# Fused attention and two-stage MLP: decode operations spread over a pair's period, phi one step later, an interleaved drain, and an earlier start for the last weight decodes

## The chip, the core and the metric

The kernel runs on one core of a Trainium2 chip. Five engines work side by side: TensorE (PE, with its weight loads listed as PEld), VectorE (DVE), ScalarE (ACT), GpSimd (POOL) and SyncE (SP), whose queue here issues nearly all transfers. The metric is device time in microseconds of one execution, lower is better.

## The reference, cut to what matters

```python
# q, k, v: (4, 8, 576, 64) f32; M_prev: (4, 8, 64, 64); z_prev: (4, 8, 64)
scores = causal(scale * q @ k.T)
a = exp(scores - scores.max(-1)); a /= a.sum(-1) + 1e-9
local = a @ v
q_p = phi(q)                      # phi(x) = where(x > 0, x, exp(x) - 1) + 1
mem_out = (q_p @ M_prev) / (q_p . z_prev + 1e-6)
x = g * mem_out + (1 - g) * local # g = sigmoid(beta), then x: (2304, 512)

h = x @ w_in                      # 512 -> 2048, float64 weights
x = (h * tanh(softplus(h))) @ w_out

a = x @ w1; b = x @ w2            # 512 -> 1024, float64 weights
out = (a * b @ w3) @ w_out2       # 1024 -> 1024 -> 512
```

The weights arrive in float64. The kernel turns each of their 128x512 tiles into float32 on the chip: this is what "decode" means below.

## The kernel before, in words

**Attention.** 32 heads are taken as 16 pairs. The loop over `p` (L514) has 17 turns: in turn `p` the scores and the softmax of pair `p` are made, and the probabilities of pair `p - 1` are transposed and multiplied by v (`pt_g`, `pv`). Scores come in blocks of rows: `s_blocks` for block 3, block 2, blocks 0 and 1, and `s_last` for the last 64 rows of both heads. For each block PE writes scores to a PSUM tile `psA`, DVE takes the masked maximum (`maxed`, L373), and ACT the exponential with its row sum (`expd`, L378). `normed` (L363 to L368) scales the rows, some on DVE and some on POOL (`ON_POOL`). `pt_g` transposes on PE into `psF`, and ACT copies the result out (L430). `pv` collects the pair's output in one `psX` and one `psF` bank; ACT copies the high part out and DVE subtracts for the low part (`sub`, L79).

**phi.** `prep_phi(p)` makes phi(q) of a pair, divided by its norm and times the gate: an exponential on ACT (L330), a GpSimd add (L331), a DVE combine (L332), a GpSimd product with z (L334), a DVE sum (L338), small steps (L339 to L341), and a GpSimd scale (L344). `trans_phi(p)` transposes the result on PE into two `psX` banks and copies it out on ACT (L351). Both were called for pair `p + 1` at the end of turn `p`, after `pv`.

**Decode.** `decode` fetches a raw tile ("draw", 512 KB, on SP's queue), runs six DVE operations on it (L113, L115, L117, L120, L124, L126) and one GpSimd addition (L131). Its user then splits the result into a rounded part (L76) and a rest (L79 or L160), both on GpSimd. `lq0` lists the eight tiles of the first quarter of `w_in` and `w_out`. `run(lq0, 1)` stood in turns 3, 6, 9 and 12, with one raw buffer; the other four tiles were decoded in turn 16, with a decoder of their own.

**First MLP.** It runs by quarters `g` of the hidden width and by chunks `n` of 384 tokens: 24 units. `emit_h` makes h in two `psA` tiles, applies tanh, arctan and sin on ACT (L477 to L485) and multiplies by h on DVE (L487). `emit_x2` multiplies by `w_out` and adds to `x2`. The first two units, (0, 0) and (0, 1), stand in turn 16 beside the last pair's work. Decodes of the next quarter run beside the units.

**Last quarter and second MLP.** Beside the units of the last quarter `fold` decodes `w3` tile by tile and multiplies it with the decoded `w_out2`, 17 steps in all. The second halves of `w2` and `w1` (eight tiles, two to a step, `rest`) are written to the place of the second half of x (`w_slot(1)`), one step in the last `emit_x2` and three beside the first blocks of the second MLP (`k < 3`). At `k == 4` the decoder's memory is given back, and the second set of x tiles (`x2s`, filled by L731 and L732) takes it.

**Order.** The framework's planner puts every engine's instructions in one fixed order when the kernel is built; emission order is its priority, and an instruction that has all it needs may be taken ahead of earlier-emitted ones. `issue_after(i)` only forbids instructions of `i`'s engine from going ahead of `i`. `in_turn` uses it to keep PE's work in emission order for turns 1 to 15.

Of the kernel before, what the change touches and what calls it, by code (L numbers as in the profile page):

```python
# [21 lines left out]
def fused_kernel(ctx: ExitStack, tc, q, k, v, M_prev, z_prev, beta, w_in, w_out, w1, w2, w3, w_out2, out):  # L22
    nc = tc.nc
# [78 lines left out]

    def decode(srcs):

        V = nc.vector
        ts = []
        for src in srcs:
            r = dec["pool"].tile([128, dec["w"], 2], I32, tag="draw", name="draw", bufs=dec["raw"])
            dm(out=r.rearrange("p n t -> p (n t)"), in_=src)
            a = dec_tile("da")  # L110
            ts.append((r[:, :, 0], r[:, :, 1], a, a.bitcast(I32), r.rearrange("p n t -> p (n t)").bitcast(F32)))
        for lw, hw, a, ai, _ in ts:
            V.tensor_scalar(out=ai, in0=hw, scalar1=0x7FFFFFFF, scalar2=None, op0=ALU.bitwise_and)  # L113
        for lw, hw, a, ai, _ in ts:
            V.tensor_scalar(out=a, in0=a, scalar1=2.0 ** -15, scalar2=122879.9921875, op0=ALU.max, op1=ALU.min)  # L115
        for lw, hw, a, ai, _ in ts:
            V.tensor_scalar(out=ai, in0=ai, scalar1=3, scalar2=0x3FFFFFF8,  # L117
                            op0=ALU.logical_shift_left, op1=ALU.bitwise_and)
        for lw, hw, a, ai, _ in ts:
            V.scalar_tensor_tensor(  # L120
                out=ai, in0=hw, scalar=-0x40000000, in1=ai, op0=ALU.bitwise_and, op1=ALU.bitwise_or
            )
        for lw, hw, a, ai, _ in ts:
            V.tensor_scalar(out=hw, in0=ai, scalar1=-0x800000, scalar2=None, op0=ALU.bitwise_and)  # L124
        for lw, hw, a, ai, _ in ts:
            V.scalar_tensor_tensor(  # L126
                out=lw.bitcast(F32), in0=lw.bitcast(U32), scalar=2.0 ** -52, in1=hw.bitcast(F32),
                op0=ALU.mult, op1=ALU.mult,
            )
        for lw, hw, a, ai, _ in ts:  # L130
            nc.gpsimd.tensor_tensor(out=a, in0=a, in1=lw.bitcast(F32), op=ALU.add)  # L131
            yield a, _
# [81 lines left out]
    decoder(at, 1, 1)  # L214
# [107 lines left out]
    def prep_phi(p):  # L322
# [15 lines left out]
        nc.vector.tensor_reduce(out=dn, in_=qz, axis=mybir.AxisListType.X, op=ALU.add)  # L338
# [10 lines left out]
    def trans_phi(p):  # L349
        t = ap_.tile([128, S], F32, tag="phi", name="phi", bufs=2)  # L350
        trans(st[p]["e"], lambda cs, o: nc.scalar.copy(out=t[:, cs], in_=o))  # L351
# [19 lines left out]

    def maxed(s, o, m, init, a):
        nc.vector.tensor_tensor_reduce(  # L373
            out=s, in0=o, in1=m, op0=ALU.add, op1=ALU.min, scale=-scale, scalar=init, accum_out=a,
        )
# [45 lines left out]
    def pt_g(p, gi):  # L421
# [8 lines left out]
        nc.scalar.copy(out=t[:, 0:n], in_=o[:, 0:n])  # L430

    def pv(p):
# [16 lines left out]
        for o, q0, q1 in ((pm, 0, 512), (pl, 512, S)):  # L449
            x = xl[b // 2][:, :, c, S * (b % 2) + q0:S * (b % 2) + q1]  # L450
            nc.scalar.copy(out=x[:, 0], in_=o[:, 0:q1 - q0])
            sub(x[:, 1], o[:, 0:q1 - q0], x[:, 0])
# [3 lines left out]
    def emit_h(u, beside=iter(())):  # L456
# [7 lines left out]
        for m in range(KQ):  # L464
# [9 lines left out]
            if m == 1:  # L474
                steps(beside, 1)
# [4 lines left out]
        first = nc.scalar.activation(out=d, in_=y[1][:, 1, 0:1], func=AF.Sin, scale=0.0)  # L480
# [3 lines left out]
        for i in range(2):  # L484
            nc.scalar.activation(out=y[i], in_=y[i], func=AF.Sin, scale=-2.0, bias=halfpi)  # L485
            for j in range(2):
                nc.vector.tensor_tensor(out=y[i][:, j], in0=y[i][:, j], in1=hp[2 * i + j], op=ALU.mult)  # L487
        return y
# [23 lines left out]
    lq0 = load_quarter(0)  # L512
    pre = predecode()
    for p in range(NPAIR + 1):  # L514

        now, old, new = p < NPAIR, p > 0, p + 1 < NPAIR
        ordered[0] = 1 <= p < NPAIR
        if old:
            ensure_x((p - 1) // (2 * NP))
        if not now:  # L520
            ek.close()
            wps[0] = wk.enter_context(tc.tile_pool(name="wp", bufs=1, side="right"))
            lk = ExitStack()
            decoder(lk, 2, 2, side="right")
        if p + 2 < NPAIR:
            load_pair(p + 2)
            load_v(p + 2)
        if now:
# [294 lines left out]
```

## Time and profile before

| what | value |
|---|---|
| median of 3 runs | 1025.31 us (1024.01 to 1026.53) |
| the profiled execution | 1024.95 us |
| its span | 1023.2 us |
| PE busy | 977.8 us, 96% |
| DVE, ACT, POOL busy | 60%, 49%, 33% |

The span goes from the first to the last instruction of the program. A busy PE is not a PE at its peak, since matmuls are pipelined; idle time on an engine costs something only where the chain of work that ends last goes through it. Times in views of the trace are counted from the start of the span.

### The profile page before, as it was taken

The page shows a single profiled execution, that of the slowest core. Times are in us where ns is not written, and L with a number is a line of the kernel's source. Part 1 is how long each engine was busy: PE and PEld are TensorE (multiplying, and loading weights), DVE is VectorE, ACT ScalarE, POOL GpSimd, SP SyncE. Part 2 cuts the span into 40 slices and gives each one's busy share as a digit, 9 for nine tenths or more (in the row PEclk, how much of TensorE's full clock was granted, in tenths as well). Part 3 has the DMA queues.
Part 4 walks back from the last instruction along what each step waited for, and adds up shares of the span by engine and source line. Part 5 has one row for each costly group of instructions (what it writes and reads, how often), then busy time and mean ns, then how long its engine had stood idle before and what let it go on. Part 6 is the DMA issues. An engine that isn't in the chain of part 4 may idle for free.

```text
span 1023.2 us, 15086 instructions
## 1 busy us (share of the span) xinstructions
PE 977.8 (96%) x5584; PEld 829.1 (81%) x5584; DVE 612.0 (60%) x1364; ACT 500.7 (49%) x1016; POOL 339.0 (33%) x345
## 2 busy tenths in 40 slices
PE   5888999999899999999999999999979999999998
PEld 2555555566799999999999999988758888888897
DVE  4887667667685759885987567667973121121111
ACT  5577888885655555556565544442313221221212
POOL 6675555433555254544454112112540000000000
PEclk9899999999999999999999999999999999999999
DMA  7343333311232124223331662222410000100101
GB/s 157 96 110 71 71 87 74 77 27 42 103 124 80 65 83 145 98 89 106 121 103 63 247 232 80 75 78 101 156 41 1 21 21 1 42 1 1 42 1 62
DMA packets 93626, 81.73 MB, mean 80 GB/s; under 512 B 68720, under 2 KB 72816, under 8 KB 93552
## 3 DMA queue, kind: packets, MB, share of 16 engines
q1 hardware_dynamic: 92224, 80.44, 25.3%
q8 instruction: 44, 0.72, 0.3%
q10 hardware_dynamic: 1328, 0.33, 0.2%
q14 instruction: 30, 0.25, 0.1%
HBM read 65.54 MB, written 15.20 MB: 79 GB/s over the span
## 4 chain that ended last, share of the span: by engine, by line
PE 71%; DVE 12%; ACT 11%; DMA 2%; POOL 2%; issue 2%; SPq 0%; POOLq 0%; ACTq 0%; DVEq 0%
PE psA L63 37%; PE psX L63 16%; PE psF L63 14%; ACT s L378 5%; ACT pt L430 3%; DVE s L368 2%; PE psF L66 2%; DMA draw<-in_moe_w_dram 1%; DVE da L120 1%; PE psX L66 1%; DVE xt L79 1%; POOL da L131 1%; DVE draw L126 1%; DVE da L117 1%; DVE s L373 1%
## 5 line engine op out<-in xcount | busy, mean ns | idle before, releaser
L63 PE MATMUL psA<-xt,wqt 128*128 128x384 f32 x1152 | 207.5, 335 | 0.2
L131 POOL TENSOR_TENSOR da<-da,draw 128x512 f32<-128x512 f32 x72 | 102.2, 1426 | 312.8 <-DVE draw L126 261.9
L63 PEld LDWEIGHTS psA<-xt,wqt 128*128 128x128 f32 x1152 | 200.0, 188 | 2.4 <-DVE y L487 0.8
L63 PE MATMUL psX<-gh,wqt 128*128 128x384 f32 x480 | 122.4, 335 | 1.1 <-DVE x L604 1.1
L749 DVE TENSOR_TENSOR bs<-bs,psA 128x512 f32<-128x512 f32 (+1 forms) x40 | 25.3, 633 | 160.0 <-ACT bs L748 160.0
L63 PE MATMUL psA<-x2h,w12t 128*128 128x512 f32 (+1 forms) x384 | 107.1, 356 | 6.9 <-DVE bs L749 4.6
L748 ACT COPY bs<-psA 128x512 f32<-128x512 f32 (+1 forms) x40 | 21.8, 545 | 162.1 <-PE psA L63 152.2
L378 ACT ACTIVATE s<-s,acc 128x512 f32<-128x512 f32 (+2 forms) x144 | 85.5, 603 | 12.8 <-DVE acc L373 12.7
L63 PE MATMUL psA<-x2s,w12t 128*128 128x512 f32 x384 | 89.6, 389 | 0.0
L63 PEld LDWEIGHTS psX<-gh,wqt 128*128 128x128 f32 x480 | 86.9, 188 | 2.3 <-DVE x L604 1.4
L477 ACT ACTIVATE y<-psA 128x384 f32<-128x384 f32 x96 | 42.0, 490 | 91.1 <-PE psA L63 91.0
L63 PEld LDWEIGHTS psA<-x2h,w12t 128*128 128x128 f32 x384 | 68.3, 189 | 20.7 <-DVE bs L749 5.0
L63 PEld LDWEIGHTS psA<-x2s,w12t 128*128 128x128 f32 x384 | 72.1, 188 | 14.9
L373 DVE CUSTOM_DVE_ANT_0 s<-psA,mask 128x512 f32<-128x512 f32 (+2 forms) x144 | 63.4, 483 | 34.4 <-PE psA L63 34.3
L63 PE MATMUL psX<-gl,wqt 128*128 128x384 f32 x240 | 80.3, 335 | 0.0
L66 PEld LDWEIGHTS psF<-ident,s 128*128 128x128 f32 x400 | 46.3, 147 | 40.8 <-ACT pt L430 24.8
L63 PE MATMUL psF<-gh,wqt 128*128 128x384 f32 x288 | 73.1, 334 | 0.0
L66 PE MATMUL psF<-ident,s 128*128 128x128 f32 x400 | 63.2, 292 | 9.9 <-ACT pt L430 7.5
L487 DVE TENSOR_TENSOR y<-y,psA 128x384 f32<-128x384 f32 x96 | 48.7, 549 | 34.9 <-ACT y L485 34.9
L63 PE MATMUL psA<-room,w12t 128*128 128x512 f32 (+1 forms) x192 | 68.0, 354 | 0.0
L368 POOL TENSOR_SCALAR s<-s,sum,ogp 128x128 f32<-128x128 f32 (+1 forms) x64 | 53.1, 840 | 37.2 <-DVE sum L364 37.2
L430 ACT COPY pt<-psF 128x512 f32<-128x512 f32 (+1 forms) x112 | 56.8, 546 | 16.0 <-PE psF L66 16.0
(114 smaller groups left out, 1878.3 us busy)
## 6 DMA issues: line engine op xcount, KB each, us to landing
draw<-in_moe_w_dram SPq DMA_DIRECT2D x32, 512.0 KB, 3.8
draw<-in_moe_w_out_dram SPq DMA_DIRECT2D x24, 512.0 KB, 3.5
draw<-in_moe_w_in_dram SPq DMA_DIRECT2D x16, 512.0 KB, 4.0
out_dram<-ob SPq DMA_DIRECT2D x18, 256.0 KB, 2.0
raw<-in_q_dram SPq DMA_DIRECT2D x32, 128.0 KB, 2.8
raw<-in_v_dram SPq DMA_DIRECT2D x32, 128.0 KB, 2.6
o_dram<-draw SPq DMA_DIRECT2D x8, 512.0 KB, 2.8
w_dram<-draw SPq DMA_DIRECT2D x8, 512.0 KB, 2.8
```

The lines of the kernel that those rows point to most:

```text
L63: tail[0] = nc.tensor.matmul(o, lhsT=l, rhs=r, start=start, stop=stop).ins
L66: tail[0] = nc.tensor.transpose(o, src, ident).ins
L79: return (eng or nc.vector).tensor_tensor(out=dst, in0=src, in1=f(hi), op=ALU.subtract)
L131: nc.gpsimd.tensor_tensor(out=a, in0=a, in1=lw.bitcast(F32), op=ALU.add)
L368: (nc.gpsimd if x in ON_POOL else nc.vector).tensor_scalar(out=s, in0=s, scalar1=d["sum"][:, x:x + 1], scalar2=og[:, x:x + 1], op0=ALU.mul ...
L373: nc.vector.tensor_tensor_reduce(out=s, in0=o, in1=m, op0=ALU.add, op1=ALU.min, scale=-scale, scalar=init, accum_out=a,)
L378: nc.scalar.activation(out=s, in_=s, func=AF.Exp, scale=-1.0, bias=a, accum_out=r)
L430: nc.scalar.copy(out=t[:, 0:n], in_=o[:, 0:n])
L477: nc.scalar.activation(out=y[m // 2][:, m % 2], in_=hp[m], func=AF.Tanh, scale=0.5)
L487: nc.vector.tensor_tensor(out=y[i][:, j], in0=y[i][:, j], in1=hp[2 * i + j], op=ALU.mult)
L748: nc.scalar.copy(out=bs, in_=pb)
L749: nc.vector.tensor_tensor(out=bs, in0=bs, in1=pa, op=ALU.mult)
```

## The change

- Decodes in attention: one tile of `lq0` in each of turns 4 to 11, fetched one turn ahead, with two raw buffers. Its six DVE operations are issued by `drip`: one after each of the four calls that make scores, the rest at the turn's end, each behind the last masked maximum emitted so far (`taken[0]`). The four decodes of turn 16 are gone.
- phi: `prep_phi(p + 1)` stays at the end of turn `p`, but its DVE operations stand behind the turn's last masked maximum, and its sum (L338) behind `pv`'s low part (`split_x[0]`). `trans_phi` is called a turn later, and its second half goes to `psF` instead of `psX`. phi of pair 0 is made at the end of turn 0 and transposed in turn 1. The last `normed` of a turn stands behind `split_x[0]` too.
- Drain (turn 16): PE's work follows emission order here as well. `emit_h` becomes a generator, and the four column blocks of unit (0, 0) are interleaved with the seven transposition groups of the last pair; the table load for sin stands behind the last copy of `pt_g`.
- Last quarter: `rest` begins in unit (3, 5), in `emit_x2` of (3, 4), alternating with `fold` (`both`): one step there, two in the last `emit_x2`, one beside the second MLP.

```diff
-    def decode(srcs):
+    def decode_ops(r):
...
+        ops = [ ... six DVE operations, one GpSimd addition, unchanged ... ]
+        return ops, a, flat
+
+    def fetch(src):
+        r = dec["pool"].tile([128, dec["w"], 2], I32, tag="draw", name="draw", bufs=dec["raw"])
+        dm(out=r.rearrange("p n t -> p (n t)"), in_=src)
+        return r
...
-    decoder(at, 1, 1)
+    decoder(at, 2, 1)
...
-    def trans(src, evac):
-        for c0, c1 in ((0, 256), (256, S)):
-            pt = psX()
+    def trans(src, evac, tags="XX"):
+        for tag, (c0, c1) in zip(tags, ((0, 256), (256, S))):
+            pt = bank(tag)
...
-        nc.vector.tensor_reduce(out=dn, in_=qz, axis=mybir.AxisListType.X, op=ALU.add)
+        with ExitStack() as k_:
+            if split_x[0] is not None:
+                k_.enter_context(tc.issue_after(split_x[0]))
+            nc.vector.tensor_reduce(out=dn, in_=qz, axis=mybir.AxisListType.X, op=ALU.add)
...
+    def drip(n):
+        if not parts and ahead:
+            r, done = ahead.pop(0)
+            ops, a, flat = decode_ops(r)
+            def last():
+                ops[6]()
+                done(a, flat)
+            parts.extend(ops[0:6] + [last])
+        with tc.issue_after(taken[0]):
+            for op in parts[:n]:
+                op()
+        del parts[:n]
...
-        ordered[0] = 1 <= p < NPAIR
+        ordered[0] = 1 <= p
...
-            lk = ExitStack()
-            decoder(lk, 2, 2, side="right")
+            h0 = h_steps((0, 0))
...
+        decodes = 4 <= p < 12
+        if 3 <= p < 11:
+            fetch_next()
         if now:
             in_turn(s_blocks, p, (3,))
+            if decodes:
+                drip(1)
         else:
-            split = split_y((0, 0), emit_h((0, 0)))
+            in_turn(next, h0)
...
-        if not now:
-            run(lq0, 2)
-            run(lq0, 2)
+            if not now:
+                in_turn(next, h0)
...
-        if p in (3, 6, 9, 12):
-            run(lq0, 1)
...
+        if now:
+            with ExitStack() as k_:
+                if old:
+                    k_.enter_context(tc.issue_after(split_x[0]))
+                normed(p, [(4, None)])
+            if decodes:
+                drip(7)
         if new:
-            prep_phi(p + 1)
-            in_turn(trans_phi, p + 1)
-        if now:
-            normed(p, [(4, None)])
+            with tc.issue_after(taken[0]):
+                prep_phi(p + 1)
+        if now and p > 0:
+            in_turn(trans_phi, p)
...
+        if last and n == NCH - 1:
+            rest = by_two(second_half(w_slot(1)))
+            beside = both(folding, rest)
...
-    rest = by_two(second_half(w_slot(1)))
-    emit_x2(prev, islice(rest, 1))
+    emit_x2(prev, rest)
```

## Rows read from the trace of the kernel before

**Rows 1.** Page, part 1: busy time and share of each engine.

```profile
PE 977.8 (96%) x5584; PEld 829.1 (81%) x5584; DVE 612.0 (60%) x1364; ACT 500.7 (49%) x1016; POOL 339.0 (33%) x345
```

**Rows 2.** Windows of attention, cut where a pair's first masked maximum starts.

```profile
core 0: us, PE busy (x) PEld busy (x) DVE busy (x) ACT busy (x) POOL busy (x), PEclk, DMA share, GB/s
12.70:26.20 13.50, 7.20 (x30) 3.86 (x31) 9.96 (x38) 9.00 (x27) 10.24 (x12) 0.83 0.73 166
26.20:97.30 71.10, 60.07 (x416) 38.29 (x416) 58.54 (x169) 47.84 (x137) 47.53 (x53) 0.89 0.37 93
82.00:97.30 15.30, 12.94 (x93) 8.51 (x90) 9.71 (x37) 11.07 (x33) 10.19 (x12) 0.89 0.31 72
97.30:208.80 111.50, 105.86 (x818) 65.96 (x816) 77.42 (x281) 93.67 (x273) 60.08 (x72) 1.00 0.34 77
208.80:221.90 13.10, 12.40 (x97) 7.46 (x96) 8.95 (x35) 10.92 (x33) 6.81 (x8) 1.00 0.10 23
221.90:236.30 14.40, 13.60 (x104) 8.43 (x105) 7.93 (x32) 11.08 (x33) 3.81 (x5) 1.00 0.03 7
```

**Rows 3.** Source line L113, first decode operation: durations min/median/max, first and last start.

```profile
L113 DVE TENSOR_SCALAR da<-draw x4: 422/426/434, 30.1 to 76.6; 128x512 int32<-128x512 int32 x4
```

**Rows 4.** Timeline of one steady pair: start, duration, operation, idle before and releaser.

```profile
119.78 0.17 DVE L363 TENSOR_SCALAR sum<-sum 128x8 f32<-128x8 f32 x1 [0.61 <-ACT s L378]
...
122.68 0.55 PE L66 MATMUL psX<-ident,phie 128*128 128x128 f32 x3 [0.35 <-DVE xt L79]
...
124.22 1.09 PE L66 MATMUL psF<-ident,s 128*128 128x128 f32 x8
124.41 0.83 DVE L332 SCALAR_TENSOR_TENSOR phie<-phie,phit 128x640 f32<-128x640 f32 x1 [1.17 <-ACT phie L330]
...
125.16 0.68 DVE L373 CUSTOM_DVE_ANT_0 s<-psA,mask 128x512 f32<-128x512 f32 x1
```

**Rows 5.** Timeline of the start: first scores, pair 0's phi, first masked maximum.

```profile
8.57 3.17 PE L63 MATMUL psA<-kt,qt 64*128 64x512 f32 x8
...
12.01 0.82 DVE L338 TENSOR_REDUCE dn<-qz 128x10 f32<-128x640 f32 x1 [3.12 <-POOL qz L334]
...
12.74 0.68 DVE L373 CUSTOM_DVE_ANT_0 s<-psA,mask 128x512 f32<-128x512 f32 x1
```

**Rows 6.** Groups by line, 0 to 420 us: decode's operations, count, busy, mean ns.

```profile
L131 POOL TENSOR_TENSOR da<-da,draw 128x512 f32<-128x512 f32 x27 | 38.8, 1445 | 90.7 <-DVE draw L126 73.6 <-issue 11.8 <-PE psA L63 5.3
...
L79 POOL TENSOR_TENSOR wqt<-da,wqt 128x512 fp32r<-128x512 f32 x20 | 25.8, 1301 | 0.5
...
L120 DVE SCALAR_TENSOR_TENSOR da<-draw,da 128x512 int32<-128x512 int32 x28 | 21.8, 799 | 0.2
...
L76 POOL TENSOR_SCALAR wqt<-da 128x512 fp32r<-128x512 f32 x20 | 12.9, 653 | 0.5
...
L113 DVE TENSOR_SCALAR da<-draw 128x512 int32<-128x512 int32 x28 | 12.7, 471 | 13.3 <-DMA draw<-in_moe_w_out_dram 5.1 <-POOL wqt L79 4.8 <-POOL s L368 1.8
```

**Rows 7.** Timeline in pair 1, GpSimd and VectorE at the same time.

```profile
31.45 1.65 POOL L334 TENSOR_TENSOR qz<-phie,zr 128x640 f32<-128x640 f32 x1 [1.71 <-DVE phie L332]
31.61 1.51 DVE L341 TENSOR_TENSOR dn<-dn,gates 128x10 f32<-128x10 f32 x1
```

**Rows 8.** Windows of the drain and of the passage to the second MLP.

```profile
677.00:717.00 40.00, 38.94 (x202) 34.74 (x202) 28.30 (x54) 11.99 (x22) 8.42 (x7) 1.00 0.25 86
717.00:768.00 51.00, 43.79 (x182) 32.91 (x182) 44.13 (x61) 13.40 (x25) 25.73 (x21) 1.00 0.29 98
248.90:277.50 28.60, 26.01 (x159) 21.69 (x160) 19.38 (x35) 14.33 (x25) 14.25 (x12) 0.94 0.22 75
```

**Rows 9.** Timeline of the drain: copies of transposed probabilities, then h's multiply.

```profile
257.67 1.08 ACT L430 COPY pt<-psF 128x512 f32<-128x512 f32 x2
...
264.69 0.55 DVE L487 TENSOR_TENSOR y<-y,psA 128x384 f32<-128x384 f32 x1
```

**Rows 10.** Chain that ended last, in order of time: start, duration, work.

```profile
243.28 4.22 PE psX L63 x20
...
285.85 8.32 PE psA L63 x48
```

**Rows 11.** Waits: engine and line, waited for, total, times, longest.

```profile
ACT x2s L731 <- POOL w12t L79: 16.9, 1, 16.9
```

More of the change, by code (lines that the diff above doesn't have):

```diff
@@ L134, in run, with decode @@
+    def decode(srcs):
+        ts = [decode_ops(fetch(src)) for src in srcs]
+        for i in range(6):
+            for ops, _, _ in ts:
+                ops[i]()
+        for ops, a, flat in ts:
+            ops[6]()
+            yield a, flat
     def run(jobs, n):
@@ L487, in emit_h @@
                 nc.vector.tensor_tensor(out=y[i][:, j], in0=y[i][:, j], in1=hp[2 * i + j], op=ALU.mult)
+        yield y
+    def emit_h(u, beside=iter(())):
+        for m, y in enumerate(h_steps(u)):
+            if m == 1:
+                steps(beside, 1)
         return y
@@ L512, in fused_kernel, with fetch_next @@
     lq0 = load_quarter(0)
+    ahead = []
+    parts = []
+    def fetch_next():
+        for src, done in islice(lq0, 1):
+            ahead.append((fetch(src), done))
+    def drip(n):
[3 more added lines that the diff above has]
+            def last():
+                ops[6]()
+                done(a, flat)
[4 more added lines that the diff above has]
+        del parts[:n]
     pre = predecode()
@@ L545, in fused_kernel @@
             in_turn(pt_g, p - 1, 2)
+            if not now:
+                in_turn(next, h0)
         if new:
@@ L551, in fused_kernel @@
             in_turn(s_blocks, p, (0, 1))
+            if decodes:
+                drip(1)
         if new:
@@ L556, in fused_kernel @@
             in_turn(pt_g, p - 1, 6)
+            if not now:
+                in_turn(next, h0)
+        if p == 1:
+            in_turn(trans_phi, 0)
         if now:
             in_turn(s_last, p)
+            if decodes:
+                drip(1)
             normed(p, [(i, e) for e in range(2) for i in range(4)])
         if p == 0:
-            in_turn(trans_phi, 0)
-        if p in (3, 6, 9, 12):
-            run(lq0, 1)
+            with tc.issue_after(taken[0]):
+                prep_phi(0)
         if old:
@@ L566, in fused_kernel @@
         if not now:
+            split = split_y((0, 0), next(h0))
             early = {(0, 1): emit_h((0, 1))}
-        if new:
-            prep_phi(p + 1)
-            in_turn(trans_phi, p + 1)
-        if now:
-            normed(p, [(4, None)])
-    lk.close()
+        if now:
+            with ExitStack() as k_:
+                if old:
+                    k_.enter_context(tc.issue_after(split_x[0]))
+                normed(p, [(4, None)])
+            if decodes:
+                drip(7)
+        if new:
+            with tc.issue_after(taken[0]):
+                prep_phi(p + 1)
+        if now and p > 0:
+            in_turn(trans_phi, p)
     at.close()
@@ L665, in w_slot, with both @@
         return t
+    def both(a, b):
+        while True:
+            next(a, None)
+            yield
+            next(b, None)
+            next(a, None)
+            yield
     folding = fold()
@@ L681, in fused_kernel @@
             w_slot(0)
+        if last and n == NCH - 1:
+            rest = by_two(second_half(w_slot(1)))
+            beside = both(folding, rest)
         if prev is not None:
-            with tc.issue_after(emit_x2(prev, folding if last and n > 0 else pre0)):
+            with tc.issue_after(emit_x2(prev, beside if last and n > 0 else pre0)):
                 split = split_y(u, y)
```

67 lines of the change are left out of this document (33 added, 34 removed).

## Prediction, made before the changed kernel was run

> **What bounds the kernel now.** I read the page's engine shares first, then the chain of work that ended last, then windows by stage, and the timeline only where the windows show loss. PE is busy nearly all of the span [rows 1], and from the drain to the end the chain is matmul after matmul; there only PE's gaps can be won. Attention is different. With no decode in it, a pair takes 111.5 / 8 = 13.94 us, and ACT, DVE and POOL are busy 11.7, 9.7 and 7.5 us of that [rows 2]: no engine is full, the chain hops from ACT to DVE to PE and back. The four pairs between 26.2 and 97.3 us took 71.1, so 17.8 each, 15.3 us more than four steady ones. All four decodes that attention holds started there, from 30.1 to 76.6 us [rows 3], though they were emitted in turns 3 to 12: the planner took them as early as their data allowed. DVE is busy 58.54 us in these four pairs against 38.7 in four steady ones, and the granted clock is 0.89 instead of 1.00 [rows 2]. So this stretch is where an order for the decodes can matter.
>
> Two smaller losses stand elsewhere. The drain, 28.6 us, holds two units' h of 8.32 us each [rows 8, 10] plus the last pair's transposes and products. The passage to the second MLP leaves PE idle 51.0 - 43.8 = 7.2 us, with DVE busy 44.1 of 51 [rows 8].
>
> **The start.** PE's first scores begin at 8.57; eight matmuls take 3.17 us, so the first block, half of them, ends near 10.2. Yet the first maximum starts at 12.74, behind pair 0's phi sum, which waited for GpSimd [rows 5]. That sum is now emitted behind the maxima. I put the first maximum at 10.5: -2.2 us. Turn 0 also loses phi's DVE work for two pairs, but has half a pair's work on other engines anyway: 13.5 becomes 12.5 (estimate), -1.0.
>
> **Pairs 1 to 3, now without decodes.** They took 82.0 - 26.2 = 55.8 us. Two at 13.75 (below) and one at 15.5: the start still leaves PE mostly idle (7.2 of 13.5 us [rows 2]), so a stretch at the lower clock level remains likely. The price of 1.5 is from the pair at 82.0, which had no more DVE work than a steady one, a clock of 0.89, and 1.35 us more time [rows 2]. Sum 43.0, so -12.8.
>
> **phi a turn later.** Two things go from a steady pair's path. PE stood 0.35 us before the second phi transposition, because its bank was the one that DVE was still reading; `psF` is free by then. And phi's combine, 0.83 us, ran just ahead of the next pair's first maximum, having waited 1.17 us for ACT [rows 4]. The pair from 208.8, in which no phi is prepared any more, took 13.1 instead of 13.94 [rows 2]: that bounds the gain at 0.85. But the work doesn't vanish: the combine now stands behind the turn's last maximum, in about the same place, and gains only if ACT's exponential comes earlier. I take a quarter, 13.75; the ends are 13.94 and 13.1. The last three pairs take 40.2 instead of 41.4: -1.2. What is late next is phi itself, and it has a whole turn to spare.
>
> **Eight pairs with a decode.** One decode is four operations like L113 (one row stands for the four; 471 ns) and two like L120 (799 ns; L126 is its like): 4 x 0.47 + 2 x 0.80 = 3.48 us on DVE. GpSimd adds 1.45 + 0.65 + 1.30 = 3.40 [rows 6]. A steady pair's DVE idles 13.94 - 9.68 = 4.26 us, so it fits by sum only: 13.16 of 13.94. By place: the first three drips come where DVE waits for PE's next scores, and cost nothing as long as it waits. The fourth (0.80) falls in the 0.61 us before the row sums [rows 4]: +0.2, on the path. The last two (1.27) fall in the 1.17 us ahead of phi's combine, which then comes after them: +0.4 for the next maximum, about half of what they and the combine take beyond that gap. Blocking between the engines adds to it: with the decodes, DVE's busy time rose by (58.54 - 38.7) / 4 = 4.95 a pair and not by 3.48, so 1.5 a decode is lost in longer instructions. A ten-element product took 1.51 us while a GpSimd product ran [rows 7]. I put a third of that on the path, 0.5: the rest of it, like the 3.40 us more of GpSimd, has slack to fall into. 13.75 + 0.2 + 0.4 + 0.5 = 14.85, say 14.8. Eight take 118.4. Before, the same eight pairs took 112.9 (from 82.0 to 97.3 + 7 x 13.94 = 194.9): +5.5. Ends: 13.94, all hidden, 111.5; and 17.8, as the four early ones, 142.4. I choose near the low end: DVE's 4.26 us of idle time is more than the 3.48 and most drips are placed in it, and a part of the 17.8 is the lower clock.
>
> The Trainium skill (SBUF — State Buffer, Who interferes with whom) speaks against the change here: a VectorE instruction with two SBUF inputs or in a two-port mode shares a port pair with GpSimd, and whoever comes second waits for the whole instruction. The trace agrees, by the 1.51 us of [rows 7]. By that rule each of the six operations may wait for a GpSimd product, which is the first rival below, 1030.6.
>
> Fetches cost SP one 512 KB issue a pair; the queue now waits a turn less for each, since there are two raw buffers: nothing.
>
> **Drain.** Two h units take 16.6 us; 25 transposes at eight in 1.09 us [rows 4] take 3.4; a pair's last products take 4.2, as the chain has them [rows 10]. That makes 24.2 of the stretch's 28.6 [rows 8], so 4.4 could go. But the second unit needs the `psA` tiles that L487 reads. Before, h ended near 256.9 (248.9 less a little, plus 8.3) and L487 came at 264.69, with two double copies of transposes of some 1.08 between [rows 9] (one row stands for both): 7.8 - 2.1 = 5.7 us of tanh, table load, arctan and sin remain, and the last products cover 4.2. PE waits 1.5 there, so -3 (2.9). Ends: 0 and -4.4. The four decodes leave the drain, where DVE was busy 19.4 of 28.6: they only made L487's neighbours longer.
>
> **Last quarter.** ACT waited 16.9 us for the last GpSimd split of `w1` before it could fill x2s [rows 11]. Two tiles move ahead of 717, where DVE has 40 - 28.3 = 11.7 us free, and two more out of k = 1 and 2. At 3.5 us of DVE a tile the end comes 7 us earlier. That could fill all of the 7.2 us gap; but part of the gap is DVE working off splits, and a `fold` step may now stand behind a pair of decodes (7 us) on DVE while PE has 8.3 us of other work. I take -4; ends -7.2 and +3.5.
>
> **Sum.** -2.2 - 1.0 - 12.8 - 1.2 + 5.5 - 3 - 4 = -18.7. The profiled execution took 1024.95, span 1023.2; so 1006.2, and the median is 0.4 above the profiled execution: **1006.6 us**. This case's own range: decode pairs of 14.2 or 15.5 (-4.8, +5.6) and the drain's and the passage's full gain or none (-1.4 and -3.2, +3 and +4), so 997 to 1019.
>
> **Rivals.**
> - *GpSimd and DVE block each other in every decode pair* (slower). Each of eight pairs then costs 17.8 as before, 3.0 more than I took: 1006.6 + 24 = **1030.6**. For it: 4.95 us of DVE a decode, 14.6 in all, is more than a steady pair. Against: part of the 17.8 was the clock. It decides from a decode pair of 14.8 + 18.7 / 8 = 17.1 us on.
> - *The lower clock comes back.* A pair at 0.89 with nothing else wrong took 1.35 more [rows 2]. Eight of them: **1017.4**. For it: the four pairs of 15 us and more, 26.2 to 97.3, had 0.89. Against: over the eight at 13.94 it was 1.00.
> - *The change doesn't do what it says*: the orders are only lower bounds, so the planner may keep phi's combine ahead of the maximum (13.94), pile the six dripped operations up at the turn's end (3.48 less the 1.17 us gap there: 13.94 + 2.3 = 16.2), and the last decodes, held by two raw buffers, end no sooner. 8 x 1.4 + 0.4 (pairs 2 and 3) + 1.2 (the last three) + 4 = 16.8 more: **1023.4**. For it: the four early decodes were taken long before the turns that they stood in. Against: each drip now has a place that it can't go ahead of, and DVE would have to be late for it to pile up.
> - *All hidden*: decode pairs 13.94 (-6.9), the five others 13.1 (-1.3 and -0.9), passage -7.2 (-3.2), drain -4.4 (-1.4): **992.9**.
>
> **How the numbers follow.** Forecast 0.57, all hidden 0.08, clock 0.10, change without effect 0.10, blocking 0.15. About 0.3% (3 us) is what a measurement can tell from no change. Blocking is slower in most of its range (0.12) and even in the rest (0.03); change without effect ends faster in part (0.04), even (0.05) or slower (0.01). Faster 0.57 + 0.08 + 0.10 + 0.04 = 0.79, same 0.08, slower 0.13. The range for 8 in 10 goes from the all-hidden case, 993, to the change without effect, 1023: above it stand most of blocking and half of that rival, below it little.
>
> **What would show it.** In the new profile: the first maximum near 10.5 us; a clock of 1.00 from the second pair on; pairs 12 to 14 at 13.7 and pairs 4 to 11 near 14.8, with DVE busy about 13.5 in them; PE's wait before the second phi transposition gone; the drain from the end of `pv(14)` about 25 us long, with PE's one wait before the second unit's h; ACT's 16.9 us wait for the last split shorter by some 7. A decode pair above 15.5 or a clock below 1.00 in them would make the forecast wrong, as would PE gaps in the `fold` steps of unit (3, 5).

## The result, and the profile after

The changed kernel takes **1031.48 us** (median of 5 runs, 1029.3 to 1031.58) against 1025.31: ratio 1.0054, interval 1.0040 to 1.0069. It is slower by 0.5%. The profiled execution took 1029.82 us, its span is 1028.0. PE's busy time hardly moved. The page's shares after, to be read against [rows 1]:

```profile
PE 976.7 (95%) x5584; PEld 829.2 (81%) x5584; DVE 614.0 (60%) x1364; ACT 502.0 (49%) x1016; POOL 337.1 (33%) x345
```

The same work is done, so the 4.8 us more of span are waiting. The windows below are cut where a pair's first masked maximum starts, like [rows 2]: the first turn, pair 1, two pairs without a decode, the eight with one, the last three, and the drain.

```profile
core 0: us, PE busy (x) PEld busy (x) DVE busy (x) ACT busy (x) POOL busy (x), PEclk, DMA share, GB/s
10.61:21.86 11.25, 7.50 (x34) 3.99 (x31) 9.23 (x32) 6.23 (x21) 4.42 (x6) 0.92 0.65 147
21.86:40.01 18.15, 16.51 (x113) 10.85 (x113) 12.56 (x43) 13.88 (x38) 13.79 (x16) 0.86 0.63 158
40.01:55.22 15.21, 13.91 (x108) 8.47 (x105) 10.76 (x37) 11.71 (x34) 7.35 (x10) 1.00 0.37 78
55.22:70.43 15.21, 13.21 (x104) 8.27 (x103) 10.76 (x37) 11.76 (x34) 7.35 (x10) 1.00 0.30 68
70.43:196.41 125.98, 108.78 (x814) 65.52 (x814) 109.67 (x327) 94.94 (x272) 84.61 (x93) 1.00 0.39 95
196.41:241.92 45.51, 40.22 (x310) 24.96 (x310) 33.41 (x110) 34.77 (x101) 25.20 (x31) 1.00 0.14 31
241.92:282.20 40.28, 35.95 (x241) 29.91 (x240) 17.41 (x52) 23.81 (x52) 6.20 (x7) 0.92 0.11 40
```

The reader is to see the third and fourth rows: pairs with no decode at all, at full clock, take 15.21 us, and before they took 13.94. A pair with a decode takes 125.98 / 8 = 15.75. By stretch, in us of the profiled executions (the drain here goes from pair 15's first maximum to the first product with `w_out`, the passage from the tanh of unit (3, 5) to the eighth block of the second MLP):

| stretch | before | predicted | after | miss |
|---|---|---|---|---|
| up to the first maximum | 12.74 | 10.5 | 10.61 | +0.1 |
| turn 0 | 13.44 | 12.5 | 11.25 | -1.2 |
| pairs 1 to 3 | 55.8 | 43.0 | 48.6 | +5.6 |
| pairs 4 to 11, one decode each | 112.9 | 118.4 | 126.0 | +7.6 |
| pairs 12 to 14 | 41.4 | 40.2 | 45.5 | +5.3 |
| drain | 41.1 | 38.1 | 40.3 | +2.2 |
| passage | 111.8 | 107.8 | 111.9 | +4.1 |

The misses add up to 23.7; span was 1028.0 where the sum gave 1004.5, 23.5 apart. So the table holds the whole of it. The chain that ended last shows a pair without a decode from inside (start, duration, work):

```profile
63.34 0.04 DVE s L390
...
63.87 0.74 DVE phie L342
64.61 0.09 DVE sum L376
64.70 0.28 POOL qz L344
64.97 1.24 issue
66.21 2.77 POOL s L381 x4
...
69.26 0.43 POOL dn L352
...
69.97 0.54 DVE dn L354
70.50 0.60 DVE s L390
```

phi, which has a whole turn to spare, is the chain: from the last maximum (L390) it goes through phi's combine (L342) and its product with z on GpSimd (L344, `qz`; the row called issue lies inside it), then GpSimd's part of the scaling (L381), the small step L352 behind that, and phi's gate product (L354), to the next pair's first maximum. In the timeline of the same stretch, start, duration, operation, idle before:

```profile
63.78 0.82 DVE L342 SCALAR_TENSOR_TENSOR phie<-phie,phit 128x640 f32<-128x640 f32 x1
64.68 1.54 POOL L344 TENSOR_TENSOR qz<-phie,zr 128x640 f32<-128x640 f32 x1 [3.46 <-DVE sum L376]
64.96 2.45 DVE L381 TENSOR_SCALAR s<-s,sum,ogp 128x256 f32<-128x256 f32 x4
66.21 2.96 POOL L381 TENSOR_SCALAR s<-s,sum,ogp 128x128 f32<-128x128 f32 x4
...
68.13 0.80 DVE L351 TENSOR_REDUCE dn<-qz 128x10 f32<-128x640 f32 x1
...
69.26 0.42 POOL L352 TENSOR_SCALAR dn<-dn 128x10 f32<-128x10 f32 x1
```

Before, the combine stood just ahead of the next pair's first maximum [rows 4]. Now it stands straight behind the last maximum, ahead of the row sums, and pulls `qz` to where VectorE and GpSimd scale the probabilities.

### The profile page after: what moved, and what is told of

Read it like the earlier page. It is cut to its first block, busy times and chain, and to the rows that moved or that the text cites. A ratio compares the mean times of both kernels' runs of the same rounds, so it can differ in the third digit from the quotient of the medians.

```text
span 1028.0 us, 15096 instructions
## 1 busy us (share of the span) xinstructions
PE 976.7 (95%) x5584; PEld 829.2 (81%) x5584; DVE 614.0 (60%) x1364; ACT 502.0 (49%) x1016; POOL 337.1 (33%) x345
## 4 chain that ended last, share of the span: by engine, by line
PE 68%; DVE 17%; ACT 7%; issue 3%; DMA 3%; POOL 3%; POOLq 0%; SPq 0%; DVEq 0%; ACTq 0%
PE psA L63 36%; PE psX L63 15%; PE psF L63 13%; ACT s L395 3%; DVE draw L121 2%; DVE s L390 2%; PE psF L66 2%; DVE da L117 2%; DVE s L381 1%; ACT pt L447 1%; DMA draw<-in_moe_w_dram 1%; DVE draw L120 1%; PE psX L66 1%; POOL s L381 1%; DVE phie L342 1%
## 5 line engine op out<-in xcount | busy, mean ns | idle before, releaser
L125 POOL TENSOR_TENSOR da<-da,draw 128x512 f32<-128x512 f32 x72 | 101.7, 1420 | 324.8 <-DVE draw L121 279.2
L66 PE MATMUL psF<-ident,s 128*128 128x128 f32 x400 | 66.3, 292 | 23.8 <-ACT pt L447 14.9
L390 DVE CUSTOM_DVE_ANT_0 s<-psA,mask 128x512 f32<-128x512 f32 (+2 forms) x144 | 62.8, 480 | 31.3 <-PE psA L63 31.1
L506 DVE TENSOR_TENSOR y<-y,psA 128x384 f32<-128x384 f32 x96 | 48.6, 549 | 53.4 <-ACT y L504 53.4
L447 ACT COPY pt<-psF 128x512 f32<-128x512 f32 (+1 forms) x112 | 59.0, 541 | 17.8 <-PE psF L66 17.8
L63 PE MATMUL psX<-wft,room 128*128 128x512 f32 x216 | 61.6, 390 | 0.4 <-DVE wft L79 0.4
```

Source lines behind the costliest of these rows:

```text
L63: tail[0] = nc.tensor.matmul(o, lhsT=l, rhs=r, start=start, stop=stop).ins
L66: tail[0] = nc.tensor.transpose(o, src, ident).ins
L125: lambda: nc.gpsimd.tensor_tensor(out=a, in0=a, in1=lw.bitcast(F32), op=ALU.add),
L390: taken[0] = nc.vector.tensor_tensor_reduce(out=s, in0=o, in1=m, op0=ALU.add, op1=ALU.min, scale=-scale, scalar=init, accum_out=a,).ins
L447: copied[0] = nc.scalar.copy(out=t[:, 0:n], in_=o[:, 0:n]).ins
```

## Experiments

All start from the changed kernel, and every ratio is against the kernel before on the same chip. "Pair" is the period of a pair without a decode; "with" that of one with a decode. Letters in the expectations: A1 is the place of `qz`, H the blocking between VectorE and GpSimd, D the raw buffers, G VectorE's load in the last quarter.

| what is different | median us | ratio (interval) | pair | with |
|---|---|---|---|---|
| nothing (after) | 1031.48 | 1.0054 (1.0040 to 1.0069) | 15.21 | 15.76 |
| phi's two orders gone | 1024.36 | 0.9991 (0.9982 to 1.0000) | 13.37 | 15.27, 16.5 |
| only the sum's gone | 1030.59 | 1.0051 (1.0031 to 1.0070) | 15.09 | 15.5, 16.2 |
| only the combine's gone | 1020.40 | 0.9945 (0.9919 to 0.9971) | 14.2 | 15.22 |
| `qz` behind the scaling | 1035.25 | 1.0099 (1.0081 to 1.0118) | 14.95 | 15.2 to 16.7 |
| `normed`'s order gone | 1036.12 | 1.0103 (1.0088 to 1.0118) | 14.86 | 16.2, 16.8 |
| phi as before | 1031.21 | 1.0056 (1.0039 to 1.0073) | 13.94 | 16.35 and more |
| drips free, phi's orders gone | 1027.02 | 1.0013 (1.0002 to 1.0025) | 13.37 | - |
| four decodes, phi's orders gone | 1019.59 | 0.9943 (0.9928 to 0.9958) | 13.37 | 15.36 |
| four, each over two turns | 1011.39 | 0.9869 (0.9855 to 0.9882) | 13.37 | 13.44 + 14.2 |
| six, each over two turns | 1007.77 | 0.9832 (0.9818 to 0.9846) | - | 13.44 + 14.2 |
| last decodes begin as before | 1031.11 | 1.0055 (1.0038 to 1.0071) | 15.23 | 15.58 |
| folded weights not split | 1027.05 | 1.0017 (1.0007 to 1.0027) | 15.22 | 15.75 |

### The orders on phi's VectorE work

**Both orders gone.**

```diff
         with ExitStack() as k_:
-            if split_x[0] is not None:
-                k_.enter_context(tc.issue_after(split_x[0]))
             nc.vector.tensor_reduce(out=dn, in_=qz, ...)
...
         if new:
-            with tc.issue_after(taken[0]):
-                prep_phi(p + 1)
+            prep_phi(p + 1)
```

> The changed kernel, with the two orders on phi's VectorE work in the turns taken away (its operations need no longer stand behind the turn's last maximum, nor its sum behind pv's subtraction); the late transposition stays. Theory A (these orders squeeze phi's VectorE work into the stretch between a pair's last and the next pair's first maximum, which is on the path): pairs without a decode fall from 15.21 to 14.2 us or less, pairs with one from 15.76 to about 14.8, the whole to 1013 to 1019 us. Theory B (the later transposition or its other bank costs the time): nothing moves, 1028 to 1032. Theory C (the order on the last normalisation costs it): nothing moves either.

A pair falls from 15.21 to 13.37 us, under what I had forecast (13.75). The time falls by 7 us only and misses theory A's 1013 to 1019: most pairs with a decode now take 16.5, and pair 1 takes 20.28 us instead of 18.15. Windows of a pair without a decode, of one with a decode, and of a slower one with a decode cut where the granted clock changes:

```profile
55.92:69.30 13.38, 13.03 (x104) 8.26 (x102) 9.88 (x37) 11.67 (x35) 7.22 (x9) 1.00 0.36 80
84.67:99.93 15.26, 12.99 (x104) 8.23 (x103) 14.33 (x42) 11.76 (x34) 10.77 (x12) 1.00 0.43 106
...
116.43:120.60 4.17, 2.06 (x19) 1.42 (x17) 3.73 (x11) 3.39 (x10) 3.71 (x4) 1.00 0.45 144
120.60:124.00 3.40, 3.40 (x15) 3.00 (x14) 2.38 (x13) 3.40 (x13) 1.86 (x2) 0.50 0.58 129
124.00:132.94 8.94, 8.94 (x74) 5.29 (x73) 8.20 (x20) 5.08 (x13) 5.23 (x6) 1.00 0.28 62
```

A decode adds 15.26 - 13.38 = 1.9 here, and in five of the eight pairs a stretch at the lower level (0.50, 1.2 GHz) adds 1.2 more. It comes after PE had only 2.06 us of work in 4.17. That is the rival "the lower clock comes back", in a kernel other than the one it was written for: in the changed kernel all these pairs run at 1.00.

**Which of the two.** The first run below takes only the first hunk of that diff, the second only the second.

> Only the order on phi's sum is taken away (it may go ahead of the last low part); the combine stays behind the last masked maximum. Theory S, the sum's order is what costs: a pair without a decode falls from 15.21 to near 13.4, as with both orders gone, and the time goes to 1024 to 1027. Theory C, the combine's order costs: such a pair stays at 14.9 to 15.2 and the time at 1030 to 1032. If the two only cost together, something between, near 14.3.

> Only the order on phi's combine is taken away (it may go ahead of the last masked maximum); the sum stays behind the last low part. Theory S: a pair without a decode stays at 14.9 to 15.2 and the time at 1030 to 1032. Theory C: it falls to near 13.4 and the time to 1024 to 1027, because the combine is then done early, the product with z ends before GpSimd's part of the scaling, and the sum, though last, waits for nothing.

It is mainly the combine's order: 14.2 without it, 15.09 without the sum's. Theory C had put the pair near 13.4, so the sum's order still costs when the combine's is gone. The second kernel is faster than the one before by 0.55%, and than theory C's 1024 to 1027, since its pairs with a decode stay at 15.22 with the clock at 1.00. Its timeline, same place in a pair:

```profile
56.63 0.94 DVE L342 SCALAR_TENSOR_TENSOR phie<-phie,phit 128x640 f32<-128x640 f32 x1
57.66 1.56 POOL L344 TENSOR_TENSOR qz<-phie,zr 128x640 f32<-128x640 f32 x1 [0.76 <-DVE phie L342]
...
63.98 0.17 DVE L376 TENSOR_SCALAR sum<-sum 128x8 f32<-128x8 f32 x1
64.43 1.45 DVE L381 TENSOR_SCALAR s<-s,sum,ogp 128x256 f32<-128x256 f32 x4
64.57 3.07 POOL L381 TENSOR_SCALAR s<-s,sum,ogp 128x128 f32<-128x128 f32 x4 [3.15 <-DVE sum L377]
66.83 0.69 DVE L79 TENSOR_TENSOR xt<-psX,xt 128x512 fp32r<-128x512 f32 x1 [0.96 <-ACT xt L468]
```

Now the combine and `qz` lie among the maxima, some seven microseconds ahead of the row sums. VectorE's four scalings take 1.45 us though GpSimd scales beside them for 3.07; in the changed kernel they took 2.45. The single instructions say why; L381 on VectorE in one pair, then L121 over all eight decodes (durations in ns: shortest, median, longest), first in the changed kernel:

```profile
L381 DVE TENSOR_SCALAR s<-s,sum,ogp x4: 334/469/1418, 65.0 to 66.9; 128x384 f32<-128x384 f32 x2, 128x256 f32<-128x256 f32 x1, 128x128 f32<-128x128 f32 x1
...
L121 DVE SCALAR_TENSOR_TENSOR draw<-draw x8: 1909/1917/1924, 80.9 to 191.3; 128x512 f32<-128x512 uint32 x8
```

and then without the combine's order:

```profile
L381 DVE TENSOR_SCALAR s<-s,sum,ogp x4: 342/444/474, 64.4 to 65.4; 128x384 f32<-128x384 f32 x2, 128x256 f32<-128x256 f32 x1, 128x128 f32<-128x128 f32 x1
...
L121 DVE SCALAR_TENSOR_TENSOR draw<-draw x8: 693/694/705, 79.4 to 186.0; 128x512 f32<-128x512 uint32 x8
```

One instruction of a group stands still for 1.0 or 1.2 us, in these groups always beside a `qz` that began before it: the scaling that begins at 64.96 and takes 1.42 ends at 66.38, 0.16 us behind `qz` (64.68 + 1.54 = 66.22). The Trainium skill (SBUF — State Buffer, Who interferes with whom) has the engine that comes second wait for the other's whole instruction, and these rows agree.

So the 1.0 us between 15.21 and 14.2 divides so: from the last maximum's end to the low part (L79) 67.33 - 63.78 = 3.55 against 66.83 - 63.98 = 2.85, and from there to the next first maximum 3.10 against 2.82, because L352 stands behind GpSimd's late scaling.

**`qz` alone moved.** `qz` is put behind GpSimd's scaling (`pooled[0]`, the last of it); everything else stays.

```diff
-        nc.gpsimd.tensor_tensor(out=qz, in0=e, in1=z..., op=ALU.mult)
+        with tc.issue_after(pooled[0]):
+            nc.gpsimd.tensor_tensor(out=qz, in0=e, in1=z..., op=ALU.mult)
```

> The changed kernel, orders on VectorE as they are, with phi's GpSimd product (qz) held behind the turn's last GpSimd normalisation. Theory A1 (the ordered combine releases the product just as the normalisations begin; GpSimd is then taken and blocks VectorE): pairs without a decode fall from 15.21 to 14.2 or less, pairs with one from 15.76 to 15.0. Theory A2 (the combine's and the sum's own time on VectorE's path is what costs): 14.9 to 15.3, and 15.5 to 16.

The scaling is back at 1.45 us, yet the pair stays at 14.95. Its timeline names the new wait:

```profile
65.80 1.45 DVE L382 TENSOR_SCALAR s<-s,sum,ogp 128x256 f32<-128x256 f32 x4
...
70.75 0.82 DVE L352 TENSOR_REDUCE dn<-qz 128x10 f32<-128x640 f32 x1 [1.43 <-POOL qz L345]
71.49 0.68 DVE L394 CUSTOM_DVE_ANT_0 s<-psA,mask 128x512 f32<-128x512 f32 x1
```

The sum waits 1.43 us for the late `qz`, and the next maximum stands behind it. So my idea (A1), that the place of `qz` alone makes the loss, is refuted: with the combine late, neither of the two places tried for `qz` is a good one.

**The last `normed` of a turn** without its order (`normed(p, [(4, None)])` bare):

> The changed kernel, with the last normalisation of a turn no longer held behind pv's subtraction. Theory C: pairs without a decode fall by 0.8 us or more, the whole to 1016 to 1021. Theories A and B: 15.2 us a pair stays within 0.3, the whole 1026 to 1032.

The pair gains 0.35 us and those with a decode lose more than that: it is not the cause. The whole, 1036.12, lies above both forecasts; four of the pairs with a decode hold a stretch at the lower level.

**phi as before**, with neither order, transposed in its own turn to two `psX` banks:

> The changed kernel with phi as it was before: prepared and transposed at the end of the turn, without orders, both halves in the old bank. The spread decodes, the drain and the last quarter stay changed. Theories A and B: pairs without a decode 13.9 to 14.0, pairs with one 15.0 to 15.5, first maximum back at 12.7, the whole 1015 to 1022. Theory C: pairs without a decode stay at 15.

The pair is 13.94, that of before. Against 13.37 this prices what "a turn later", with its second bank, is worth without the orders: 0.57 us a pair. The rest of the forecast failed: pairs with a decode take 16.35 us and more instead of 15.0 to 15.5, and the whole 1031.21 instead of 1015 to 1022. So the spread decodes beside the old phi are slower than the kernel before.

### The decodes

**The drips' order.** With phi's orders gone, the decode operations also lose theirs, so the planner may take them when their data are there.

```diff
-        with tc.issue_after(taken[0]):
-            for op in parts[:n]:
-                op()
+        for op in parts[:n]:
+            op()
```

> The kernel of e1 without the order that holds each dripped decode operation behind the last maximum emitted. Theory M (the order is what spreads them): pairs with a decode take 17 us or more, the whole 1032 or more. Rival N (the planner's own order does as well or better): within 3 us of e1's 1024.4, or faster.

All eight GpSimd additions then begin between 35 and 127 us and pair 1 takes 29 us. 1027.02 against 1024.36: the order does spread the decodes, as theory M says, but it is worth 2.7 us and not 7.6 or more; that is inside what rival N allowed.

**Half a decode at a time**, both orders of phi gone: pair 12 gets GpSimd's three operations of a decode and nothing else, pair 13 VectorE's six. These are extra operations on data that nothing uses; one execution, 1024.92 us.

> The kernel of e1 plus test work whose results nobody uses: three GpSimd operations like a decode's last three beside turn 12 (one extra trio, no VectorE part), and one more decode's six VectorE operations, dripped in the same places, in turn 13 (no GpSimd part). In e1 these pairs took 13.37 and 13.38 us, a pair with a whole decode 15.3 at the full clock. Theory H (blocking between the two engines makes the cost): each half alone adds under 0.7. Theory I (VectorE's time by itself): the VectorE half adds 1.4 or more, the GpSimd half under 0.3. Theory J (GpSimd is the late one): the GpSimd half adds 1.2 or more.

```profile
198.75:213.47 14.72, 12.61 (x92) 8.46 (x90) 9.87 (x36) 10.98 (x33) 11.25 (x13) 0.88 0.28 64
213.47:227.26 13.79, 13.43 (x106) 8.51 (x106) 12.77 (x42) 12.08 (x35) 7.61 (x9) 1.00 0.12 27
```

VectorE's half adds 13.79 - 13.38 = 0.41. GpSimd's pair takes 1.34 more, with a stretch at the lower level in it; the pairs of the next run that hold such a stretch and no decode take 14.5 to 14.67, so by that comparison GpSimd's half adds about 0.1. This is one pair, and its three operations were taken 4 to 9 us into the pair, where a real decode's stand at the end. What shows H is VectorE's timeline at the end of a pair: first the pair of 15.26 with a whole decode (both orders gone), with the GpSimd addition that runs there, then pair 13 with VectorE's half alone:

```profile
97.14 1.72 DVE L379 TENSOR_SCALAR s<-s,sum,ogp 128x576 f32<-128x576 f32 x1
98.78 1.23 DVE L342 SCALAR_TENSOR_TENSOR phie<-phie,phit 128x640 f32<-128x640 f32 x1
97.26 1.28 POOL L125 TENSOR_TENSOR da<-da,draw 128x512 f32<-128x512 f32 x1
...
226.03 0.58 DVE L379 TENSOR_SCALAR s<-s,sum,ogp 128x576 f32<-128x576 f32 x1
226.53 0.82 DVE L342 SCALAR_TENSOR_TENSOR phie<-phie,phit 128x640 f32<-128x640 f32 x1
```

The last scaling stands still beside the addition (L125) and the combine beside the rounding behind it (L76, 98.63 to 99.33): 1.14 + 0.41 = 1.55 us. The two pairs differ by 15.26 - 13.79 = 1.47, so most of the 1.9 is that the two engines meet (H).

**Four decodes in attention** (turns 4, 6, 8, 10), four in the drain as before, phi's orders gone:

```diff
-        decodes = 4 <= p < 12
-        if 3 <= p < 11:
+        decodes = p in (4, 6, 8, 10)
+        if p + 1 in (4, 6, 8, 10):
             fetch_next()
```

> The kernel of e1 with only four decodes in attention, in turns 4, 6, 8 and 10; the other four stand in the drain, by twos with two raw buffers, as in the kernel before. If a decode costs a pair 1.9 to 3.1 us and consecutive ones bring the lower clock (theory K): the pairs with one stay at 15.2 to 15.4 with the clock at 1.00, the last pair starts near 224, the drain is 1 to 4 us longer than e1's 39.3, the whole 1011 to 1016. Rival L (a decode in the drain costs as much there as in a pair): 1020 to 1025.

Decode pairs cost 1.99, at a clock of 1.00 as theory K has it, and three of the four turns after one cost about 1.2 in lower clock. The time, 1019.59, lies between K's range and L's: from pair 15's first maximum to unit (3, 5)'s first tanh this kernel takes 435.9 us, the one without decodes in the drain 430.5, so a decode costs 1.3 there.

**Each decode over two turns**, three operations a turn, one behind each of the first three calls that make scores; none behind the last maximum. First four over turns 4 to 11 (four in the drain), then six over turns 3 to 14 (two in the drain), as the diff has it:

```diff
-        decodes = 4 <= p < 12
-        if 3 <= p < 11:
+        decodes = 3 <= p <= 14
+        if 3 <= p + 1 <= 14 and (p + 1 - 3) % 2 == 0:
             fetch_next()
...
             in_turn(s_last, p)
-            if decodes:
-                drip(1)
...
-            if decodes:
+            if decodes and (p - 3) % 2:
                 drip(7)
```

> The kernel of e7 with each of its four decodes spread over two turns of 4 to 11: three operations in the first, three and the GpSimd trio in the second, and none behind the last maximum. If blocking beside the normalisations and the fall of the clock behind a decode pair cost the time (theories H and K): pairs of 13.6 to 14.2 at a clock of 1.00, the last pair near 221, the whole 1012 to 1016. Rival (the planner or the clock makes it no better): 1018 to 1022.

> As e11, but with six decodes spread over turns 3 to 14 and only two in the drain. With pairs at 13.9 this is 2 us longer in attention and 0 to 2 us shorter in the drain than e11: 1012 to 1018; if each half costs 0.8 us or more it is 4 us or more slower than e11.

With six, a turn that holds the second half of a decode and its GpSimd operations, then one that holds the first half of the next decode:

```profile
69.36:83.57 14.21, 13.85 (x108) 8.57 (x106) 13.06 (x40) 12.50 (x36) 10.69 (x12) 1.00 0.49 121
83.57:97.01 13.44, 12.33 (x100) 7.96 (x98) 11.40 (x40) 11.07 (x34) 7.40 (x9) 1.00 0.36 81
```

A decode now costs 14.21 + 13.44 - 2 x 13.37 = 0.91, nearly all of it in the turn with the GpSimd operations, and the clock stays at 1.00. The edit halves VectorE's work in a turn and moves GpSimd's operations away from the turn's end at once; which of the two saves the other microsecond was not separated. **1007.77 us is the best of all, 1.7% under the kernel before**, and 23.7 us under the changed one. Of the 16.6 us of span that it gains on before, 14.9 are there at pair 15's first maximum (221.35 against 236.28) and 2.1 in the drain (39.0). Both kernels came in under their forecasts, and six was to be no faster than four: attention is 1.7 us longer, as said, but from pair 15's first maximum to unit (3, 5)'s first tanh six take 430.1 us and four 434.7, for fewer decodes are left in the drain.

### The last quarter

**The last decodes begin where they did before** (`rest` made after the loop, one step in the last `emit_x2`):

```diff
-        if last and n == NCH - 1:
-            rest = by_two(second_half(w_slot(1)))
-            beside = both(folding, rest)
...
-    emit_x2(prev, rest)
+    rest = by_two(second_half(w_slot(1)))
+    emit_x2(prev, islice(rest, 1))
```

> The changed kernel with the decodes of the second halves of w1 and w2 at their old place (the last emit_x2 and the first three blocks). Theory D (the earlier start is eaten up: the decodes and the fold share two raw buffers, so the last one ends hardly sooner): within 2 us of the changed kernel. Rival E (the early start costs by itself, other things hide it): 3 us or more faster. Rival F (it gains as forecast and the loss is elsewhere): 4 us slower.

1031.11 against 1031.48, passage 112.2 against 111.9: in all, the early start is worth nothing (D). Two things cancel there. Behind unit (3, 5)'s first tanh the last split begins at 92.3 us in the changed kernel and at 94.3 in this one. But from the end of that split to the first matmul with `x2s` the changed kernel takes 18.0 us, this one and the kernel before 16.4: only the changed one holds a half-clock stretch there, 3.4 us from 771.0.

**One tile a step in place of two** (`run(jobs, 1)` twice):

> The changed kernel with the two tiles of each step of the second halves decoded one after the other instead of operation by operation together. Theory D (both raw buffers come free together, so fetch and decode don't overlap): the last split of w1 comes 3 us or more earlier, the stretch from unit (3, 5)'s first tanh to the eighth block of the second MLP falls from 111.9 to 107 to 109, the whole 3 to 5 us faster than the changed kernel. Rival G (VectorE is simply full there, or the fold comes late): within 1.5 us of the changed kernel.

1031.5, ratio 1.0061 (1.0044 to 1.0078). The planner put the splits at the same places, so this edit changed nothing and tells nothing about the raw buffers (D). A third raw buffer was not tried; that part stays open.

**Less for VectorE beside the last decodes**: the subtraction for the low part of the folded weights is left out.

```diff
-                sub(wft[:, 1, i], f(wft[:, 1, i]), wft[:, 0, i])
```

> The changed kernel without the eight VectorE subtractions that make the low part of the folded weights (the second MLP then multiplies by a wrong low part). Theory G (VectorE is full in the passage, so the last decodes wait for it): the stretch from unit (3, 5)'s first tanh to the eighth block falls from 111.9 to 107 to 109.5, and the last split comes 3 us or more earlier. Theory D (two raw buffers set the pace): within 1.5 us.

The kernel leaves that low part out. The passage falls from 111.9 to 107.4. The wait for the last split of `w1`, first in the changed kernel,

```profile
ACT x2s L811 <- POOL w12t L79: 13.6, 1, 13.6
```

then without the subtraction:

```profile
ACT x2s L811 <- POOL w12t L79: 10.4, 1, 10.4
```

The last split begins 2.9 us earlier after unit (3, 5)'s tanh (764.5 - 675.0 against 765.7 - 673.4), just under the 3 us forecast, and the half-clock stretch of 3.4 us at 771.0 in the changed kernel is gone: 16.4 us from the split's end to `x2s` instead of 18.0. These two make the 4.5. So VectorE's load (G) holds the last split back by 2.9 us, more than the 2.0 that beginning earlier gains.

## Why the prediction was wrong

**The step that failed** is in "phi a turn later": "the combine now stands behind the turn's last maximum, in about the same place", hence 13.75 with 13.94 as the upper end. Counted from the pair's first maximum it stood at 124.41 - 111.20 = 13.2 us before and stands at 63.78 - 55.22 = 8.6 now, 4.6 us earlier than I took, between the last maximum and the row sums, where the scaling waits behind it. I read an order as a lower bound in my rivals and as a place in my sum. I also said of phi that it "has a whole turn to spare": true of its result, not of the engines' queues that its operations stand in. The measured pair is 15.21; 1.46 us over 13.75, in two early pairs 2.9 and in eight later ones 11.7, and the last three pairs show the same (+5.3). That is 19.9 of the 23.7 us. The runs show both parts: 1.0 by the combine's order alone, 0.8 more by the sum's once the combine's is gone (14.2 to 13.37), and 0.1 by the sum's alone; the two are not additive.

**The idea under that step was right and undersized**: transposing a turn later, without the orders and with the second bank, is worth 0.57 us a pair where I took 0.2.

**A decode** was priced at 14.8 - 13.75 = 1.05 on the path. In the changed kernel it adds 15.75 - 15.21 = 0.54, probably because the pair already waits for `qz`, which saves 8 x 0.5 = 4.1 of the miss; over a pair of 14.2 it adds 1.0 (15.22), over one of 13.37 it adds 1.9. The term holds only for the slack that it was made with. Its last two drips did not lie where I had them either, in the gap ahead of the combine. They too were taken as early as their order let them, ahead of the scaling (L120 at 96.16, L121 at 96.63, the scaling at 98.47), and there L121 met `qz`. And 471 and 799 ns were means with blocked instructions in them: unblocked, as with both orders gone, the two kinds take 0.42 and 0.69 us.

**The start** came as said (first maximum 10.61 for 10.5), turn 0 better by 1.2. **Pair 1** holds 5 us at the lower level (0.86 in its row) and takes 18.15; I had 15.5, from a pair with a shorter stretch. That is 2.6 us of the miss. 5 us at half the clock cost 2.5 at most (an estimate), 1.0 more than my 1.5; the rest is the longer pair again.

**Drain.** PE's one wait was where I put it, and 2.2 us instead of 1.5. What I left out came behind it. Rows of the timeline, around the second unit's h:

```profile
271.16 1.95 DVE L506 TENSOR_TENSOR y<-y,psA 128x384 f32<-128x384 f32 x4 [15.65 <-ACT y L504]
272.24 4.08 PE L63 MATMUL psA<-xt,wqt 128*128 128x384 f32 x13 [2.20 <-DVE y L506]
```

and the windows from 268 us on, the last of them the half-clock stretch:

```profile
268.00:272.24 4.24, 2.04 (x39) 1.40 (x35) 1.08 (x3) 4.23 (x7) 0.00 (x0) 1.00 0.00 0
272.24:272.70 0.46, 0.46 (x3) 0.46 (x4) 0.46 (x2) 0.46 (x3) 0.00 (x0) 1.00 0.00 0
272.70:276.10 3.40, 3.40 (x12) 3.40 (x12) 3.40 (x7) 2.61 (x3) 0.00 (x0) 0.50 0.00 0
```

The h of 48 matmuls takes 10.15 us instead of the 8.32 of [rows 10]. The changed kernel's drain holds one more such stretch, from 245.4, whose cause no run shows; the drain before held one, from 264.0. Two kernels without any have drains of 37.2 (phi as before) and 37.5 (no order on the combine), 3.9 and 3.6 under before; two with one, like before, have 39.0 (no order on the sum) and 39.4 (both gone), 2.1 and 1.7 under it. So the interleaving is worth some 2 us of the 3 that I said at an equal number of stretches, and the second stretch gives most of it back.

**Last quarter.** The first split came 10.5 us earlier after unit (3, 5)'s tanh, the last only 1.6, and ACT's wait fell from 16.9 [rows 11] to 13.6, not by 7. The working counted VectorE's free time ahead of 717 and then treated it as given to the decodes; the fold's own work moved back instead (its last `w3h` copy from 49.4 to 54.6 us behind that tanh). The 1.6 that was left went to the half-clock stretch at 771.0, and the passage is unchanged.

**The rivals.** *GpSimd and DVE block each other* gave 1030.6, close to the time by chance: decode pairs are 15.76, under the 17.1 from which it was to decide, and pairs without a decode miss my figure by more (1.46 us against 0.96). Blocking is real, but here most of it comes from phi's `qz`. *The change doesn't do what it says* (1023.4) holds in part: the last decodes end hardly sooner, as it says, and orders did act as lower bounds only, but they let the combine and the last drips come early, where it had the drips pile up late. *The lower clock* shows in the decode pairs of several other kernels here, first of the one without both orders, not in this one's.

## What to carry to other kernels

An order that says "not before X" doesn't keep an operation near where it was: it may now be taken straight behind X, so look at who else becomes free at that moment, on its engine and on the engine it feeds. Work with a whole period of slack should be ordered by the place it is to have, among operations that wait for something else anyway. And where two engines block each other, look at which instructions of the main path a side job's operations lie beside, and try it over two periods: the same decode cost 1.9 us in one turn and 0.9 over two.

## What the runs showed of the hardware

- Blocking between VectorE and GpSimd went both ways. VectorE's four scalings took 1.45 us beside GpSimd's own scalings (3.07 us of TENSOR_SCALAR) that began after them, and there GpSimd's 128x512 took 0.98 us, against 0.77 for the one behind them. In the changed kernel they took 2.45, for the first began inside one TENSOR_TENSOR (`qz`, 1.54 us) and waited to its end. It is not the TENSOR_TENSOR kind alone: in that kernel's pairs with a decode the 128x576 scaling takes 1.13 us instead of 0.58, beside a GpSimd TENSOR_SCALAR (L341, 87.24 to 87.97).
- Short waits of PE in an otherwise busy stretch were followed by 3.4 us at 0.50 (1.2 GHz): after 2.06 us of work in 4.17, and after 2.04 in 4.24. These two cost 1.2 and 1.8 us, so a wait of about 2 us on PE can cost as much again. It need not: pairs of one length differ, for those of 15.22 us without the combine's order show no such stretch in eight, and those of 15.26 without both orders lead to one (and to 16.5) in five of eight. PE's wait of 3.05 us in the passage was followed by one in the changed kernel (from 771.0), and by none in the kernel before.
